# Sliding-window attention with sinks, then a mixture of four experts, on one core: the first q and k rows read in runs of four tokens, turned by transposes of 64x64, and the order of issue refitted

## The chip, the cores and the metric

The kernel runs on one core of a Trainium2 chip. The metric is the device time of one execution in microseconds; the kernel before takes 358.95 us (median of 3 runs, 358.85 to 359.42).

## What is computed

Four batches, eight heads, 768 tokens, head dimension 64. Each query sees the 128 latest keys and the first four tokens (the sinks). The attention output is laid out as 3072 tokens by 512 and goes through four experts, each a matrix of 512 by 1024, a ReLU and a matrix of 1024 by 512, mixed by normalized gates.

```python
scores = scale * np.matmul(q, k.transpose(0, 1, 3, 2))
keep = is_sink | ((rel >= 0) & (rel < window))      # rel = query position - key position
a = softmax(np.where(keep, scores, -1e9))
x = (a @ v).transpose(0, 2, 1, 3).reshape(B * S, H * D)
p = domain_probs / (domain_probs.sum(-1, keepdims=True) + 1e-09)
for e in range(E):
    out += p[:, e:e + 1] * (np.maximum(x @ w1[e], 0.0) @ w2[e])
```

## The kernel before

**Work.** A batch is cut into three groups of 256 tokens (g = 0, 1, 2) and a group's heads into four pairs (hp = 0 to 3). For each pair and group the attention of batch 0 runs through these steps: `transposes` (q and k turned so that the head dimension lies on the partitions, L594 to L600, and copied from PSUM to qkT, L613), `scores` (L706, in group 0 with a mask added by a matmul with the identity, L700), the exponential on ScalarE (L746), `values` (L786, sinks L779), reciprocal and scaling on VectorE (L813, L816), and `turn` (L847), which puts the tokens' features back on the partitions as xT. Later batches are turned by DMA transposes instead. The experts' first products take xT and w1 (L1106, for the first groups; L1189, in a form with seven products instead of eight, for the rest), their second products H and w2 (L1433, and L1358 in the seven-product form).

**First rows.** `load_first` (L287) reads group 0 of batch 0 as fp32: four DMAs of 256 KB, two for q on SP's queue and two for k on ACT's. Each takes four heads; partition p holds tokens 2p and 2p+1 of each head, so a packet is 512 bytes. `cast_first` (L308) casts each half to bf16 in the tiles `first`, q on VectorE and k on ScalarE (both recorded at L302). For hp 0 and 1 the first half is enough, hp 2 and 3 need the second. `transposes` turns, for each hp, 128 partitions by 128 columns (two heads of 64) for each of q and k and each of the two token parities: four transposes of 128x128, written to two PSUM banks (one for q, one for k), then one copy on VectorE (q) and one on ScalarE (k) that puts the tokens back in order.

**Other loads.** All other rows of batch 0, the values tiles vx and the weights are read by GpSimd's software DMA queue, in the order vx 0 and 1, q and k rows of group 1, vx 2, the first quarter of w1 of expert 0, vx 3, the other quarters, w2 of expert 0, and so on (L521 to L531). SP's queue also carries the gate probabilities (L457, L505) and the values of the sinks (vsf, L502, eight small DMAs).

**Start of the other engines.** VectorE and ScalarE first make the identity, and the masks (L535 to L565; ScalarE's two activations L544 and L545 make a term of the second mask, and a table load stands ahead of them). TensorE runs idle products (L574, into an accumulator that is not used yet) from its first instruction on: nine of 512 columns (L1464), and then one of 256 columns whenever the planner sees nothing ready within 220 ns (L1550).

**Order.** The order of all instructions is fixed when the program is built, by a planner that keeps an assumed clock for each engine (`t`, L108) and the assumed landing times of DMAs (`landed`). In each round (L1494) it picks the next TensorE work from options with priorities, and puts the other engines' work into a list with a ready time and an allowed delay (`later`, L163), from which `flush` (L167) emits it. The landing times of the first rows are numbers written out in `load_first` (L298), the times at which VectorE and ScalarE come free are set at L548. The block of constants from L60 to L113 holds the priorities, delays and shares: for example `GATE` and `GATE0` (allowed delay of the gated ReLU), `FORM` and `FORM2` (of the sums of weights for the seven-product form), `LOW_PRODUCT`, `HIGH_PRODUCT`, `LOW_SECOND`, `EARLY` and `OPEN` (priorities), `SHARE_OF` and `LEAD` (how far the attention of a batch runs ahead of the experts), `FLIP` (a delay put on transposes of groups 1 and 2).

Of the kernel before, what the change touches and what calls it, by code (L numbers as in the profile page):

```python
# [11 lines left out]
FP32 = mybir.dt.float32  # L12
BF16 = mybir.dt.bfloat16
# [3 lines left out]
def kernel(  # L17
# [12 lines left out]
    nc = tc.nc  # L30

    B, H, S, D = q.shape
# [5 lines left out]
    P = 128  # L38
# [6 lines left out]
    NQB = S // P  # L45
    NHP = H // 2
# [5 lines left out]
    G = 2 * P  # L52
# [5 lines left out]
    ]  # L58

    NGATE = 5  # L60
    START = {0: (1, 0), 1: (0, 1), 2: (0, 0), 3: (0, 0)}
    DENSE = 2
    NT3 = 3
    MIX = 4
    SHARE_OF = (0.634, 1.111, 1.102)
    LEAD = (1.272, 0.235)
    DUE = 0
    LOW_PRODUCT = 2.791
    LOW_SECOND = 4.402
    HIGH_PRODUCT = 0.207  # L70
    EARLY = 0.154
    GATE = 8921
    GATE0 = 5401
    FORM = 20576
    FORM2 = 37391
    TOKEN00 = 33179
    TOKEN0 = 1119
    WAIT2 = 16164
    WAIT1 = 5898
    LATE3 = 3  # L80
    TOKEN = 11155
    MARGIN = 494
    FULL = 7
    STEP0 = 0.141
    READY = 46
    WIDE = 2
    OPEN = 1.198
    ONACT = 1
    ONE = 2
    PAIR = 1  # L90
    SINK2 = 1
    PAD = 198
    MASKD = 99999999
    GROW = 24662
    ONLY2 = 1
    BEHIND = 7198
    CHORES = 2
    OWN = 2
    BIASED = 1
# [8 lines left out]
    t = {"pe": 1200.0, "act": 0.0, "dve": 0.0, "pool": 1280.0, "sp": 800.0, "sw": 6500.0, "hw": 0.0}  # L108
    ring, whole = [0.0] * 6, [False] * 6
    WARM = 6600.0  # L110
    FLIP = 421
    LATE = 259
    LATE1 = 12449  # L113

    def pe(cols, *deps, n=1, switch=0):
        t["pe"] = max([t["pe"], *deps])
        rate = 2.4 if t["pe"] > WARM else 1.2
        t["pe"] += cols / rate + 2.5 * n + 95 * switch
        return t["pe"] + 215
# [47 lines left out]
    def flush(until, once=False):  # L167

        ran = False
        while True:  # L170
            best = None
            for engine in ("act", "dve", "pool"):
                mine = [x for x in pend if x[2] == engine or x[2] == "any" and engine != "pool"]
                if not mine:
                    continue
                at = max(t[engine], min(x[0] for x in mine))
                if at <= until and (best is None or at < best[0]):
                    best = at, engine, min((x for x in mine if x[0] <= at), key=lambda x: x[1])
            if best is None:
                return ran  # L180
            pend.remove(best[2])
            t[best[1]] = best[0]
            best[2][3](best[1])
            ran = True
            if once:
                return True
# [14 lines left out]
    landed = {}  # L201
# [32 lines left out]
    sb = ctx.enter_context(tc.tile_pool(name="attn_sb", bufs=2))  # L234
    mo = ctx.enter_context(tc.tile_pool(name="moe_sb", bufs=2))
# [9 lines left out]
    nat = {}  # L245
# [40 lines left out]

    def load_first():  # L287

        raw = {name: mo.tile([P, 2, 4, 2 * D], FP32, name=f"{name}raw", tag=f"wide{i}", bufs=1) for i, name in enumerate("qk")}
        for half in range(2):  # L290
            hs = slice(4 * half, 4 * half + 4)
            for name, src in (("q", q), ("k", k)):
                x = raw[name][:, half]
                (nc.sync if name == "q" else nc.scalar).dma_start(
                    out=x, in_=src[0, hs, 0:G, :].rearrange("h (p t) d -> p h (t d)", t=2),
                )
                nat[0, half, name, "raw"] = x
            landed["first", half] = ((4870.0, 5180.0), (7550.0, 7350.0))[half]  # L298
            t["sp"] += 530

    def copy(engine, out, in_):
        (nc.scalar.copy if engine == "act" else nc.vector.tensor_copy)(out=out, in_=in_)  # L302

    first = {name: sb.tile([P, 2, H, D], BF16, name="qkn", tag="qkn", bufs=NQB) for name in "qk"}
    qkn_free[-2:] = [1e12] * 2
    cast_at = {}

    def cast_first(half):  # L308
        hs = slice(4 * half, 4 * half + 4)

        def cast(at):
            cast_at[half] = at

        part = join(2, cast)
        for i, name in enumerate("qk"):
            def run(engine, i=i, name=name):
                copy(
                    engine, first[name][:, :, hs, :],
                    nat[0, half, name, "raw"].rearrange("p h (t d) -> p t h d", t=2),
                )  # L320
                part(clock(engine, 512))
            later(("dve", "act")[i], landed["first", half][i], 0, run)
# [130 lines left out]
    pr = scratch[:, 4 * P:4 * P + E * NT].rearrange("p (j e) -> p j e", e=E)  # L453
# [46 lines left out]
    for h in range(H):  # L500
        r = 32 * (h // 2) + NSINK * (h % 2)
        nc.sync.dma_start(  # L502
            out=vsf[r:r + NSINK, :, 0:D], in_=v[:, h, 0:NSINK, :].rearrange("b j d -> j b d"),
        )
    nc.sync.dma_start(out=pr, in_=moe_domain_probs.rearrange("(p j) e -> p j e", p=P))  # L505
    ident = consts.tile([P, P], BF16, name="ident")
    for sgn in (1, -1):
        nc.gpsimd.affine_select(
            out=identf, in_=identf, compare_op=ALU.is_ge, fill=0.0,
# [5 lines left out]
    for base, sgn in ((0, 1), (NSINK - 1, -1)):  # L515
        nc.gpsimd.affine_select(
            out=sel2, in_=sel2, compare_op=ALU.is_ge, fill=0.0, base=base,
# [10 lines left out]
    for i in range(1, 4):  # L528
# [11 lines left out]
        out=low[0].rearrange("p (n q) -> p n q", n=3)[:, 0::2], in0=two, scalar1=LOW, scalar2=-LOW, op0=ALU.mult, op1=ALU.add,  # L540
# [4 lines left out]
    nc.scalar.activation(out=low[1][:, P:2 * P], in_=own, func=AF.Copy, scale=LOW, bias=-LOW)  # L545
    mask0 = consts.tile([P, 3 * P], BF16, name="mask0")
    mask1 = consts.tile([P, 2 * P], BF16, name="mask1")
    t["dve"] = t["act"] = 4600.0  # L548
    cast_first(0)
    flush(4700.0)  # L550
    for x in vx:
        nc.vector.memset(x[:, :, D:DX], 1.0)
    t["dve"] += 240.0

    vsd = {}
    half = consts.tile([P, 2], BF16, name="half")
# [6 lines left out]
        nc.vector.memset(x, 0.0)  # L563
    for x, y in zip((mask0, mask1), low):
        nc.vector.tensor_scalar(out=x, in0=y, scalar1=1 / LOW, scalar2=1.0, op0=ALU.mult, op1=ALU.add)  # L565
    t["dve"] += 400.0
    cast_first(1)

    acc = [psum.tile([P, 2 * G], FP32, name=f"acc{i}", tag=f"o{i}", bufs=1) for i in range(2)]

    def idle_products(x, n, cols=2 * G):

        for _ in range(n):
            nc.tensor.matmul(x[:, 0:cols], lhsT=zeros[:, 0:P], rhs=zeros[:, 0:cols], start=True, stop=True)  # L574
            pe(cols)
# [5 lines left out]
    def transposes(b, g, hp):  # L581

        if b not in qkT:
            qkT[b] = sb.tile([P, 2, NHP, S], BF16, name="qkT", tag="qkT", bufs=1)
        ready = max(cast_at[hp // 2] if (b, g) == (0, 0) else rows_at(b, g), free_at(2 if (b, g) == (0, 0) else 1))
        slots, trs = [], []
        for i in range(2 if (b, g) == (0, 0) else 1):
            slots.append(pick())
            trs.append(bank(slots[i], [P, 2, 2, P], BF16, "tr"))
            ring[slots[i]] = 1e12  # L590
        hs = slice(2 * hp, 2 * hp + 2)
        for i in range(2):
            for tt in range(2):
                if (b, g) == (0, 0):  # L594
                    nc.tensor.transpose(trs[i][:, i, tt], first["qk"[i]][:, tt, hs], ident)
                    continue
                for ph in range(2):
                    nc.tensor.transpose(
                        trs[0][64 * ph:64 * ph + 64, i, tt], nat[b, 2 * g + i][:, 2 * hp + ph, tt * D:(tt + 1) * D], ident,
                    )  # L600
        done = pe(4 * P, ready, n=4, switch=0 if (b, g) == (0, 0) else 2)
        dst = qkT[b][:, :, hp, g * G:(g + 1) * G]

        def copied(at):
            for slot in slots:
                take(slot, at)
            turned_at[b, g, hp] = at

        if (b, g) == (0, 0):
            part = join(2, copied)  # L610
            for i, engine in enumerate(("dve", "act")):
                def run(engine, i=i):
                    copy(engine, dst[:, i].rearrange("c (p t) -> c p t", t=2), trs[i][:, i].rearrange("c t p -> c p t"))  # L613
                    part(clock(engine, 2 * P))
                later(engine, done, 0, run)
        else:
            def run(engine):
                copy(engine, dst.rearrange("c i (p t) -> c i p t", t=2), trs[0].rearrange("c i t p -> c i p t"))
                copied(clock(engine, 4 * P))
            later("any", done, 300, run)  # L620
        if hp == NHP - 1:
            for _ in range(2):
                qkn_free.remove(1e12)
                qkn_free.append(done)
            qkn_free.sort()
# [835 lines left out]

    idle_products(acc[1], 9)  # L1464
    mix = Mixture()
    att = Attention(0)
    work = [
# [2 lines left out]
    ahead, upto, loaded, wide = 0, 0.0, 0, 0  # L1470
# [23 lines left out]
    while mix.more() or att.more():  # L1494
        now = t["pe"]

        if not att.more() and ahead == B - 1 and not wide:
            wide = 1
# [16 lines left out]
        x = next((x for x in loads if load_ready(x) < now + 1500), None)  # L1515
# [3 lines left out]
        if turns and (ahead < 2 or not mix.second) and landed.get(("qk", *turns[0]), 1e12) < now and (turns[0][0] <= ahead or turns[0][0] == ahead + 1 and not att.todo):  # L1519
            x = turns.pop(0)  # L1520
            turn_nat(*x)
            b = x[0]
# [18 lines left out]
        s2, p = mix.second_ready(), mix.product_ready()  # L1541
# [10 lines left out]
        if soonest > 1e11:  # L1552
            if loads:
                x = loads.pop(0)
# [50 lines left out]
```

## Time and profile before

| | us |
|---|---|
| median of 3 runs | 358.95 |
| the profiled execution's own time | 358.95 |
| its span, first to last instruction | 357.2 |
| TensorE busy | 348.8 (98%) |
| VectorE busy | 306.7 (86%) |
| ScalarE busy | 168.7 (47%) |
| GpSimd busy | 70.5 (20%) |
| first transposes of the first rows start (L595) | 5.83 |
| values tiles 0 and 1 landed | 8.28, 9.32 |
| last matmul starts | 353.18 |

The profile shows one execution. Its page gives each engine's busy time, the span in 40 slices, the DMA queues, the chain of work that ended last and the costliest groups of instructions; further views answer for a stretch of time, a line or a tile. The granted clock of TensorE is 1.00 throughout. PE is TensorE's matmuls, PEld its weight loads, DVE VectorE, ACT ScalarE, POOL GpSimd, SP the engine that only issues DMAs. Packet and completion times come from the same trace: q0 is GpSimd's software queue, q1 SP's and q10 ACT's hardware queue. The largest shares of the chain that ended last are the experts' products: 35% at L1189, 31% at L1358 and 7% at L1433.

### The profile page before, as it was taken

To read this page: it belongs to the slowest core of one execution; us is meant where nothing else is said; L and a number is where in the kernel's file an instruction comes from. 1 tells how busy PE (TensorE), PEld (TensorE's weight loads), DVE (VectorE), ACT (ScalarE), POOL (GpSimd) and SP (SyncE) were. 2 spreads that over 40 slices of the span, in tenths; PEclk is the share of its full clock that TensorE was granted. 3 is DMA by queue.
4 is the path that set the end of the run, shared out by engine and by line. 5 is a ranking of instruction groups with operands and counts; after the bars stand their busy time and mean duration, and the time that the engine had idled before them with its cause. 6 is when DMAs were issued, how large, how long until landed. Compare 5 with 4: busy or idle time off the path is not lost.

```text
span 357.2 us, 11108 instructions
## 1 busy us (share of the span) xinstructions
PE 348.8 (98%) x4673; PEld 302.6 (85%) x4673; DVE 306.7 (86%) x701; ACT 168.7 (47%) x432; POOL 70.5 (20%) x90
## 2 busy tenths in 40 slices
PE   8999999999999999999999999999999999999995
PEld 3675687777688998998998998899899999999884
DVE  6669999998799899899699799699799699999630
ACT  5866451437882922566444722926443632322110
POOL 8934114311260440420030620000000000000000
PEclk9999999999999999999999999999999999999999
DMA  9999999999993999691086999124112221100011
GB/s 175 185 195 203 230 210 174 137 135 139 227 148 42 138 168 157 75 119 46 32 68 111 148 156 139 50 54 55 44 32 63 59 52 51 37 31 31 1 61 60
DMA packets 115318, 37.86 MB, mean 106 GB/s; under 512 B 97196, under 2 KB 110764, under 8 KB 115268
## 3 DMA queue, kind: packets, MB, share of 16 engines
q0 software_dynamic: 74416, 17.31, 55.4%
q1 hardware_dynamic: 39796, 19.32, 29.3%
q8 instruction: 36, 0.59, 0.7%
q10 hardware_dynamic: 1056, 0.52, 0.6%
q14 instruction: 14, 0.11, 0.1%
HBM read 41.03 MB, written 6.34 MB: 133 GB/s over the span
## 4 chain that ended last, share of the span: by engine, by line
PE 83%; DVE 6%; ACT 5%; DMA 2%; issue 1%; POOL 1%; DVEq 0%
PE cps L1189 35%; PE acc L1358 31%; PE acc L1433 7%; PE hps L1106 3%; PE sps L706 3%; ACT onat L825 2%; PE od L786 2%; ACT aT L746 2%; DMA vx<-in_v_dram 2%; DVE H L1223 1%; DVE cps L1239 1%; DMA gates<-gate_rows 1%; PE od L779 1%; DVE onat L816 1%; DVE H L1254 1%
## 5 line engine op out<-in xcount | busy, mean ns | idle before, releaser
L1189 PEld LDWEIGHTS <-w 128*128 128x128 bf16 x1408 | 87.1, 98 | 3.5 <-issue 1.0
L1358 PEld LDWEIGHTS <-H 128*128 128x128 bf16 x720 | 66.6, 98 | 7.9 <-issue 1.2
L1223 DVE SCALAR_TENSOR_TENSOR H<-cps,gates 128x512 bf16<-128x512 f32 x105 | 69.8, 683 | 0.0
L1358 PE MATMUL acc<-w,H 128*128 128x256 bf16 x432 | 56.8, 273 | 0.1
L1189 PE MATMUL cps<-xT,w 128*128 128x128 bf16 x704 | 52.5, 219 | 0.5 <-ACT onat L825 0.5
L1189 PE MATMUL cps<-T,w 128*128 128x128 bf16 x704 | 52.5, 219 | 0.1
L746 ACT ACTIVATE aT<-sps 128x512 bf16<-128x512 f32 (+1 forms) x96 | 46.5, 571 | 9.7 <-PE sps L706 9.5
L1232 ACT COPY cps<-cps 128x512 f32<-128x512 f32 x44 | 25.7, 592 | 44.2 <-PE cps L1189 33.8
L1405 ACT COPY osb<-acc 128x256 f32<-128x256 f32 x40 | 15.4, 384 | 59.2 <-PE acc L1358 59.2
L825 ACT ACTIVATE onat<-od,R 128x64 bf16<-128x64 f32 x144 | 32.8, 349 | 21.7 <-DVE R L813 21.7
L1358 PE MATMUL acc<-wf,H 128*128 128x256 bf16 x288 | 39.3, 273 | 0.0
L1189 PEld LDWEIGHTS <-qkn 128*128 128x128 bf16 x576 | 34.8, 98 | 1.1 <-issue 0.2
L1239 DVE TENSOR_TENSOR cps<-H,cps 128x512 f32<-128x512 f32 x40 | 27.7, 691 | 9.0 <-PE cps L1189 6.2
L1358 PEld LDWEIGHTS <-S 128*128 128x128 bf16 x320 | 30.2, 98 | 4.2 <-issue 1.0
L1245 ACT COPY H<-cps 128x512 f32<-128x512 f32 x40 | 23.7, 600 | 18.1 <-PE cps L1189 18.1
L1433 PE MATMUL acc<-w,H 128*128 128x512 bf16 x128 | 30.1, 379 | 0.0
L1189 PEld LDWEIGHTS <-vf 128*128 128x128 bf16 x480 | 28.8, 98 | 0.1
L331 POOL DMA_DIRECT2D vx<-in_v_dram x24 | 21.4, 909 | 37.4 <-PE od L786 25.9
L1254 DVE TENSOR_TENSOR H<-H,cps 128x512 f32<-128x512 f32 x40 | 27.0, 680 | 1.7 <-PE cps L1189 1.6
L271 POOL DMA_DIRECT2D rows<-in_q_dram x18 | 16.0, 887 | 61.1 <-DMA qkT<-rows 51.0
L1189 PE MATMUL cps<-T,qkn 128*128 128x128 bf16 x384 | 27.3, 219 | 0.1
L727 DVE TENSOR_TENSOR aT<-aT,mask 128x1024 bf16<-128x1024 bf16 (+1 forms) x36 | 22.8, 641 | 1.9 <-ACT aT L746 1.6
(123 smaller groups left out, 524.2 us busy)
## 6 DMA issues: line engine op xcount, KB each, us to landing
w<-in_moe_w_dram POOLq DMA_DIRECT2D x7, 1024.0 KB, 23.1
out_dram<-osb SPq DMA_DIRECT2D x23, 256.0 KB
gates<-gate_rows SPq DMA_DIRECT2D x40, 128.0 KB
vx<-in_v_dram POOLq DMA_DIRECT2D x24, 128.0 KB, 10.0
rows<-in_q_dram POOLq DMA_DIRECT2D x18, 128.0 KB, 6.4
rows<-in_k_dram POOLq DMA_DIRECT2D x18, 128.0 KB, 6.7
w<-in_moe_w_dram POOLq DMA_DIRECT2D x4, 256.0 KB, 8.4
kraw<-in_k_dram ACTq DMA_DIRECT2D x2, 256.0 KB
```

The lines of the kernel that those rows point to most:

```text
L331: nc.gpsimd.dma_start(out=vx[tb][:, :, 0:D], in_=v[b, :, tb * P:(tb + 1) * P, :].rearrange("h p d -> p h d"),)
L727: nc.vector.tensor_mul(x, x, m[:, None, :].to_broadcast([P, n, 2 * w // n]))
L746: nc.scalar.activation(out=a[:, ph], in_=sps[ph][:, 0:w], func=AF.Exp, scale=scale)
L825: nc.scalar.mul(o[:, qi, hp, ph * D:(ph + 1) * D], od[:, qi, ph, 0:D], R[:, qi, ph])
L1189: nc.tensor.matmul(y[:, f], lhsT=A[:, d, f * P:(f + 1) * P], rhs=T[:, d], start=(m in ("P1", "P5") and f == 0 and d == 0), stop=(d == 1), ...
L1223: nc.vector.scalar_tensor_tensor(out=dst, in0=src, scalar=0.0, in1=gate, op0=ALU.max, op1=ALU.mult)
L1232: nc.scalar.copy(out=tiles["Y"], in_=y)
L1239: nc.vector.tensor_add(tiles["V"], c5, tiles["X"])
L1245: nc.scalar.copy(out=c5, in_=y)
L1254: nc.vector.tensor_add(c5, c5, y)
L1358: nc.tensor.matmul(x, lhsT=self.operand(b, g, e, m)[:, f], rhs=forms[e][m][:, f], start=(k == 0 and f == 0 and m in (("P1", "P5", "P2") if ...
L1433: nc.tensor.matmul(op, lhsT=H[:, fb // QF, fb % QF, s], rhs=w2_sb[e][:, fb, :], start=(fb == 0), stop=(fb == NFB - 1),)
```

## The change

The first rows are read in runs of four tokens: partitions 0 to 63 take the even heads of the half and partitions 64 to 127 the odd ones, partition p of a half holding tokens 4p to 4p+3. Each DMA therefore covers 64 partitions and two heads, with packets of 1024 bytes, and there are eight instead of four. The casts copy without a change of order. For each hp, each of q and k is turned by eight transposes of 64x64, two (one on each half of the partitions) for each of the four tokens of a run, in the same two PSUM banks; the copies after them put four tokens in order instead of two. The casts of the first half are entered in the planner's list after the masks, its assumed landing times and engine times are new constants (`FIRST`, `BEGIN`), the idle products at the start become six (`NIDLE`), and some 25 of the planner's other constants get new values.

```diff
+    RUN = 4
+    FIRST = ((3980.0, 3950.0), (5500.0, 5450.0))
+    BEGIN = (4400.0, 4000.0)
+    NIDLE = 6
...
-    SHARE_OF = (0.634, 1.111, 1.102)
-    LEAD = (1.272, 0.235)
+    SHARE_OF = (0.61, 1.111, 1.102)
+    LEAD = (1.272, 0.328)
...
-    LOW_PRODUCT = 2.791
-    LOW_SECOND = 4.402
-    HIGH_PRODUCT = 0.207
-    EARLY = 0.154
-    GATE = 8921
-    GATE0 = 5401
+    LOW_PRODUCT = 2.872
+    LOW_SECOND = 4.475
+    HIGH_PRODUCT = 0
+    EARLY = 0.207
+    GATE = 9087
+    GATE0 = 5108
...
-    FORM2 = 37391
+    FORM2 = 43794
...
-    FLIP = 421
+    FLIP = 34
...
-        raw = {name: mo.tile([P, 2, 4, 2 * D], FP32, ...) ...}
+        raw = {name: mo.tile([P, NHP, RUN * D], FP32, ...) ...}
         for half in range(2):
             hs = slice(4 * half, 4 * half + 4)
             for name, src in (("q", q), ("k", k)):
-                x = raw[name][:, half]
-                (nc.sync if name == "q" else nc.scalar).dma_start(
-                    out=x, in_=src[0, hs, 0:G, :].rearrange("h (p t) d -> p h (t d)", t=2),
-                )
+                x = raw[name][:, 2 * half:2 * half + 2]
+                rows = src[0, hs, 0:G, :].rearrange("(n h) (p t) d -> h p n (t d)", h=2, t=RUN)
+                for ph in range(2):
+                    (nc.sync if name == "q" else nc.scalar).dma_start(out=x[64 * ph:64 * ph + 64], in_=rows[ph])
...
-            landed["first", half] = ((4870.0, 5180.0), (7550.0, 7350.0))[half]
+            landed["first", half] = FIRST[half]
+            t["sp"] += 530
             t["sp"] += 530
...
-    t["dve"] = t["act"] = 4600.0
-    cast_first(0)
-    flush(4700.0)
     for x in vx:
         nc.vector.memset(x[:, :, D:DX], 1.0)
-    t["dve"] += 240.0
...
-    t["dve"] += 400.0
+    t["dve"], t["act"] = BEGIN
+    cast_first(0)
     cast_first(1)
...
+            if (b, g) == (0, 0):
+                x = trs[i][:, i].rearrange("c t p -> c (t p)").rearrange("c (t p) -> c t p", t=RUN)
+                for tt in range(RUN):
+                    for ph in range(2):
+                        pr = slice(64 * ph, 64 * ph + 64)
+                        nc.tensor.transpose(x[pr, tt], first["qk"[i]][pr, hp, tt], ident[pr, pr])
+                continue
             for tt in range(2):
-                if (b, g) == (0, 0):
-                    nc.tensor.transpose(trs[i][:, i, tt], first["qk"[i]][:, tt, hs], ident)
-                    continue
...
-                    copy(engine, dst[:, i].rearrange("c (p t) -> c p t", t=2), trs[i][:, i].rearrange("c t p -> c p t"))
+                    x = trs[i][:, i].rearrange("c t p -> c (t p)")
+                    copy(engine, dst[:, i].rearrange("c (p t) -> c p t", t=RUN), x.rearrange("c (t p) -> c p t", t=RUN))
...
-    idle_products(acc[1], 9)
+    idle_products(acc[1], NIDLE)
```

The other constants that move, old value first: TOKEN0 1119, 1517; WAIT2 16164, 15046; WAIT1 5898, 5930; TOKEN 11155, 12447; MARGIN 494, 154; FULL 7, 8; STEP0 0.141, 0.15; READY 46, 17; OPEN 1.198, 0.991; GROW 24662, 24255; BEHIND 7198, 7891. The planner also counts two changes of TensorE's tile shape for the first transposes, which it counted as none.

More of the change, by code (lines that the diff above doesn't have):

```diff
@@ L64 @@
     MIX = 4
-    SHARE_OF = (0.634, 1.111, 1.102)
-    LEAD = (1.272, 0.235)
+    SHARE_OF = (0.61, 1.111, 1.102)
+    LEAD = (1.272, 0.328)
     DUE = 0
-    LOW_PRODUCT = 2.791
-    LOW_SECOND = 4.402
-    HIGH_PRODUCT = 0.207
-    EARLY = 0.154
-    GATE = 8921
-    GATE0 = 5401
+    LOW_PRODUCT = 2.872
[4 more added lines that the diff above has]
+    GATE0 = 5108
     FORM = 20576
-    FORM2 = 37391
+    FORM2 = 43794
     TOKEN00 = 33179
-    TOKEN0 = 1119
-    WAIT2 = 16164
-    WAIT1 = 5898
+    TOKEN0 = 1517
+    WAIT2 = 15046
+    WAIT1 = 5930
     LATE3 = 3
[L81 to L85, printed above, removed]
+    TOKEN = 12447
+    MARGIN = 154
+    FULL = 8
+    STEP0 = 0.15
+    READY = 17
     WIDE = 2
-    OPEN = 1.198
+    OPEN = 0.991
     ONACT = 1
@@ L93 @@
     MASKD = 99999999
-    GROW = 24662
+    GROW = 24255
     ONLY2 = 1
-    BEHIND = 7198
+    BEHIND = 7891
     CHORES = 2
@@ L287, in load_first @@
     def load_first():
-        raw = {name: mo.tile([P, 2, 4, 2 * D], FP32, name=f"{name}raw", tag=f"wide{i}", bufs=1) for i, name in enumerate("qk")}
+        raw = {name: mo.tile([P, NHP, RUN * D], FP32, name=f"{name}raw", tag=f"wide{i}", bufs=1) for i, name in enumerate("qk")}
         for half in range(2):
@@ L302, in copy @@
         (nc.scalar.copy if engine == "act" else nc.vector.tensor_copy)(out=out, in_=in_)
-    first = {name: sb.tile([P, 2, H, D], BF16, name="qkn", tag="qkn", bufs=NQB) for name in "qk"}
+    first = {name: sb.tile([P, NHP, RUN, D], BF16, name="qkn", tag="qkn", bufs=NQB) for name in "qk"}
     qkn_free[-2:] = [1e12] * 2
@@ L308, in cast_first @@
     def cast_first(half):
-        hs = slice(4 * half, 4 * half + 4)
         def cast(at):
@@ L317, in run @@
                 copy(
-                    engine, first[name][:, :, hs, :],
-                    nat[0, half, name, "raw"].rearrange("p h (t d) -> p t h d", t=2),
+                    engine, first[name][:, 2 * half:2 * half + 2],
+                    nat[0, half, name, "raw"].rearrange("p h (t d) -> p h t d", t=RUN),
                 )
@@ L600, in transposes @@
                     )
-        done = pe(4 * P, ready, n=4, switch=0 if (b, g) == (0, 0) else 2)
+        done = pe(4 * P, ready, n=4, switch=2)
         dst = qkT[b][:, :, hp, g * G:(g + 1) * G]
```

## Prediction

> **What bounds the kernel now.** I read the page first, its busy times and its slices:
>
> ```profile
> PE 348.8 (98%) x4673; PEld 302.6 (85%) x4673; DVE 306.7 (86%) x701; ACT 168.7 (47%) x432; POOL 70.5 (20%) x90
> ...
> PE   8999999999999999999999999999999999999995
> ```
>
> TensorE is filled from the first slice to the last; the reader is to see that a change can win only where PE is idle, late to start, or fed with fillers. PE is idle for 357.2 - 348.8 = 8.4 us. The table of windows puts 1.85 of it in 0 to 10 us, 0.40 in 10 to 20, 0.85 in 20 to 30, 0.27 in 30 to 40, 3.55 after 300 (nearly all of it the last store, behind the last matmul) and about 1.5 over the 260 us between. To this come the fillers of L574: 21 matmuls, 1.92 us before 5 us and 1.28 between 5 and 16, if counted at the later rate (L1433: 512 columns in 216 ns). So the head is where the change can act, and I asked for the chain of waits of the first 30 us alone:
>
> ```profile
> 2.53 0.99 POOL vx L331
> 3.52 5.80 DMA vx<-in_v_dram
> 9.36 0.26 PE od L786 x3
> ...
> 22.29 0.44 DVE onat L816
> 22.77 0.30 PE tx L847 x2
> 23.09 0.38 ACT xT L302
> 23.52 2.45 PE hps L1106 x21
> ```
>
> Columns: start, length, what. The head is a chain that starts with a software DMA (the first two values tiles, landing at 9.32), runs over VectorE and ScalarE, and gives the bound to PE only at 23.5. The timeline shows the other input, the first q and k rows:
>
> ```profile
> 1.94 1.28 ACT L544 ACT_TABLE_LOAD   x1 [1.94 <-issue]
> ...
> 4.48 0.43 DVE L302 CAST qkn<-qraw 128x512 bf16<-128x512 f32 x1
> ...
> 4.93 0.62 ACT L302 CAST qkn<-kraw 128x512 bf16<-128x512 f32 x1 [1.19 <-DMA kraw<-in_k_dram]
> ...
> 5.83 0.61 PE L595 MATMUL tr<-ident,qkn 128*128 128x128 bf16 x8
> ...
> 6.81 0.57 DVE L302 CAST qkn<-qraw 128x512 bf16<-128x512 f32 x1
> 7.03 0.62 ACT L302 CAST qkn<-kraw 128x512 bf16<-128x512 f32 x1
> ```
>
> The k casts start as their rows land (4.91 and 7.00, from the completions in the trace). The first q cast starts as VectorE comes free (masks until 4.46; q landed at 4.46). The second q rows landed at 6.11, and their cast stood behind two copies. Last, the windows of half a microsecond (columns: length, busy time of each engine, clock, DMA share, GB/s):
>
> ```profile
> 2.00:2.50 0.50, 0.50 (x3) 0.15 (x1) 0.47 (x2) 0.50 (x1) 0.43 (x3) 1.00 0.51 116
> 2.50:3.00 0.50, 0.50 (x2) 0.15 (x1) 0.39 (x4) 0.50 (x1) 0.50 (x2) 1.00 0.59 154
> ...
> 3.50:4.00 0.50, 0.50 (x3) 0.21 (x2) 0.42 (x5) 0.25 (x2) 0.50 (x2) 1.00 1.15 344
> ...
> 5.50:6.00 0.50, 0.50 (x8) 0.45 (x7) 0.00 (x0) 0.05 (x1) 0.50 (x1) 1.00 1.30 298
> ```
>
> The rows come slowly for the first microsecond, then at 344 GB/s; the last packet starts at 6.08. The first software packet starts at 5.78, though GpSimd issued it at 2.49. Later in the trace, where that queue had been empty, the first packet came 1.6 to 2.2 us after the issue. So the values wait for the first rows to get off the 16 DMA engines, and from then on the software stream has no gap until 89 us.
>
> **The change, part by part.**
>
> *Rows in runs of four tokens.* 2048 packets of 512 B become 1024 of 1024 B. In this trace hardware packets of 512 B take 27 ns at best, other ones of 1024 B (stores, gates) 44 at the lower quarter and 49 at the median. At best: 2048 x 27 / 16 = 3.46 us against 1024 x 44 / 16 = 2.82, 0.64 saved. In the slow first microsecond the packets come at 226 to 268 per us, and only the SP queue's until 2.86; if packets and not bytes are what is limited there, doubling their size moves those 135 KB in half the time, 0.4 saved. Bounds: 0 (344 GB/s is a limit of bytes, and the ramp is time) to 1.2. I take 0.9, near the sum, since the ramp's rows are so far under the later ones: last packet at about 5.2.
>
> *Eight issues instead of four.* SP and ACT each issue two more. An issue of 512 packets took 0.45 to 0.58, one of 16 packets (vsf) 0.25 to 0.30, a store of 128 packets 0.34; the new ones carry 128, so I take 0.36. ACT: 4 x 0.36 = 1.44 for 1.10, so the table load and the two activations behind it come 0.35 later and end at 4.1. Behind them VectorE's last mask waits: it began at 3.86 and took 0.60, to 4.46, and GpSimd's issue ended at 4.43, so it may well have waited for that. Up to 0.4 on ACT is then free. At 0.55 an issue, ACT ends at 4.85 and mask and q cast slip by 0.7 or more: that end is kept for the range. On SP the two issues stand ahead of the probabilities and vsf, and these will wait for semaphores of the first rows as the vsf issues already do (3.0 us for kraw). Their readers come at 13.9 (vsd) and 25.9 (gates), issues end at 8.4 now: nothing, with 5 us of cover.
>
> *First half.* The q cast cannot start before 4.46, as now; the k cast starts at 4.1 instead of 4.93. Both are over by 4.9 instead of 5.55. The idle products must not stand in the way: nine of 512 columns at 0.43 us end near 5.3, six end at 4.0, and the planner adds short ones up to the rows. First transposes 5.83 to about 5.05: 0.8 earlier.
>
> *Transposes of 64x64.* 64 instead of 16. The 16 start 56 ns apart. The nearest row for small ones is L598 (64 columns loaded, 128 moved): 0.64 us for 16, the last 0.22 being latency, 28 ns apart. 64 x 28 = 1.8 us for 0.9; between 25 and 56 ns apart it is +0.7 to +2.7 us of PE, partly in idle time. A change of shape ahead of L706 costs about 0.25 of weight-load idle (4.5 us in 18); I allow two or three more. On the chain that is 0.2 to 0.3 for each half.
>
> [...]
>
> *Second half and copies.* Rows land near 5.9 instead of 7.0. The casts then stand behind the first copies, not behind the DMA, and end about 6.5 instead of 7.65. hp 2 and 3 are scored a microsecond earlier, so the first values wait for vx alone. The copies keep their size (0.37 to 0.43).
>
> *Software stream.* It starts as the rows leave the engines: 5.78 less 0.9, no earlier than 2.49 + 2.2 = 4.7. GpSimd issues far ahead (5.8 us from issue to landing at first, 9.2 at the last w1 piece), so vx (9.32), w1 (14.61 to 19.36) and w2 (24.47) all come 0.9 earlier, and the pieces under PE's later work move with it.
>
> *Order.* Some 25 numbers of the planner move a little. Between 40 and 350 us PE is idle for only 1.5 us, so a new order can win at most about that; it can lose as much in stalls at the handovers between batches (near 98, 121 and 221 us the chain already leaves PE). I take 0, bounds -0.7 to +1.2.
>
> *Sum.* -0.9 (stream and rows) -0.5 (hp 2 and 3 no longer late) +0.3 (transposes on the chain) + 0 = -1.1 us of the profiled execution's 358.95 (span 357.2 and 1.75 around it), which is also the median of the runs shown: 357.85.
>
> **Rivals.**
>
> *A. The stream does not move, or the head's gain is given back.* If the first software packet at 5.78 is the queue's own start-up, vx stays at 9.32 and w1 where it is; only hp 2 and 3 gain, 0.2 to 0.4: 358.6. For it: the first k packet too came late, at 2.86. Against it: the 1.6 to 2.2 us of later issues. The same time results if VectorE (95% busy from 30 to 60 us) cannot follow.
>
> *B. Slower: pieces of 64 partitions at half rate.* If writes to one half of the partitions get half the engines' rate (344 / 2 = 172 GB/s), and q and k ask for the same half at once, 1.05 MB take 6.1 us, the last packet starts near 8 instead of 6.08, and the second rows land near 8.9. hp 2 and 3 slip by 1.9, the stream by 1 to 2. With 0.5 of the slip taken up by work at hand: about +1.2, 360.1. It decides as soon as the eight pieces average under 250 GB/s. Against it: k starts later than q, so the two may write different halves.
>
> [...] No row of this trace has such a piece, so it stays open here.
>
> *C. Slower: the new order stalls at a handover.* One more stall like those near 98 or 121 us (aT and onat on ACT, 1.6 and 2.5 long) with the head's 1.1 gained: +0.8 net, 359.8. Decides once PE idle between 40 and 350 us exceeds 1.5 by more than the head's gain.
>
> **How the numbers follow.** Forecast (-0.6 to -2.0): 0.58. A: 0.20. B: 0.08. C: 0.14. A time within 0.2% (0.72 us) is about what a measurement of this kernel cannot tell from no change; the edges are 358.23 and 359.67. Nearly all of the forecast lies below, A between, B and C above mostly: 0.58 faster, 0.22 same, 0.20 slower. The forecast's own range is 356.9 to 358.3; with A and part of C, 356.7 to 359.8 leaves out less than 2 in 10.
>
> **What would show it.** Right: kraw completions near 4.0 and 5.9, first software packet near 4.9, first 64x64 transposes near 5.05, vx at 8.4, first hps products of the second group (22.89 now) before 22. Wrong: a first packet still at 5.8 (A), second rows after 7 (B), the q cast after 5 (the issues), PE idle over 2.5 us between 40 and 350 (C).

## The result, and the profile after

The kernel after takes 363.59 us (median of 5 runs, 362.81 to 363.88) against 358.95 for the kernel before (5 runs, 358.55 to 359.42): a ratio of 1.012, 95% interval 1.0106 to 1.0134. That is 4.6 us slower, where 1.1 us faster was forecast and 356.7 to 359.8 was the range. The profiled execution has a span of 362.2 us for 357.2. The page of the kernel after:

```profile
PE 349.3 (96%) x4710; PEld 302.7 (84%) x4719; DVE 306.2 (85%) x701; ACT 169.1 (47%) x432; POOL 68.5 (19%) x90
...
PE   4898999999989999999999999999999999999996
...
PEclk9699999999999999999999999999999999999999
```

TensorE is busy for nearly as long as before (349.3 for 348.8), so 4.5 of the 5.0 us are idle time. The reader is to see the first slice at 4 (it was 8) and, what the page before did not have, a granted clock of 6 tenths in the second slice. Line numbers have moved: from the masked scores on they are higher by five (L711 is L706 of before), the helper of casts and copies is L307 (L302), the first transposes are L598 (L595). The chain of waits of the first 32 us (start, length, what):

```profile
3.15 6.51 DMA qraw<-in_q_dram
9.76 0.44 DVE qkn L307
10.24 0.64 PE tr L598 x16
10.88 0.75 PE sps L705 x2
...
14.44 0.45 PE od L791 x6
...
28.83 2.45 PE hps L1111 x21
```

The head no longer hangs on the values tiles but on the last piece of the first q rows. The first values products come at 14.37 in the timeline (8.85 before), and the products that end the head at 28.83 instead of 23.52: 5.3 us late. The last matmul starts at 358.78 instead of 353.18, so the loss is made in the head, and the rest adds 0.3. The timeline of the head:

```profile
3.52 1.28 ACT L547 ACT_TABLE_LOAD   x1 [3.52 <-issue]
...
6.42 0.87 DVE L307 CAST qkn<-qraw 128x512 bf16<-128x512 f32 x1 [0.84 <-DMA qraw<-in_q_dram]
...
7.34 0.69 PE L598 MATMUL tr<-ident,qkn 64*64 64x64 bf16 x32 [2.31 <-DVE qkn L307]
...
9.76 0.43 DVE L307 CAST qkn<-qraw 128x512 bf16<-128x512 f32 x1 [2.47 <-DMA qraw<-in_q_dram]
...
10.10 1.08 DVE L307 COPY qkT<-tr 128x256 bf16<-128x256 bf16 x3
...
10.81 0.82 PE L705 MATMUL sps<-lent,ident 128*128 128x384 bf16 x2
...
14.37 0.51 PE L791 MATMUL od<-vx,aT 128*128 128x65 bf16 x6
```

A mask product pair and the first values products of the kernel before, for comparison:

```profile
6.38 0.49 PE L700 MATMUL sps<-lent,ident 128*128 128x384 bf16 x2
...
8.85 0.25 PE L786 MATMUL od<-vx,aT 128*128 128x65 bf16 x3
```

Three things are to be seen. ScalarE's table load starts at 3.52 instead of 1.94. The rows come late: q casts at 6.42 and 9.76 instead of 4.48 and 6.81. And VectorE's copies of the first two pairs, turned by 8.0, start at 10.10: on VectorE they stand behind the second half's cast. Windows (length, busy times of PE, PEld, DVE, ACT and POOL, clock, DMA share, GB/s), first of the kernel before, then two of the kernel after:

```profile
5.00:10.00 5.00, 4.56 (x47) 2.57 (x45) 2.32 (x7) 3.88 (x10) 5.00 (x7) 1.00 1.97 193
```

```profile
5.00:10.00 5.00, 0.72 (x33) 0.58 (x32) 1.33 (x3) 1.56 (x5) 4.42 (x6) 0.79 1.85 183
10.00:15.00 5.00, 4.76 (x52) 1.84 (x54) 1.26 (x5) 3.19 (x9) 3.31 (x5) 0.53 1.85 177
```

From 5 to 10 us TensorE has 0.72 us of work (4.56 before). From 10 to 15 it looks busy, at half its clock: two mask products take 0.82 us (L705) where they took 0.49 (L700).

The clock column needs a warning. The trace's clock entries are 1.00 from 4.50 us, 0.50 from 7.91 and 1.00 again from 14.73. They begin with the first change, and for the time before it the views count 1.00, which the matmuls contradict: idle products of 512 columns start 0.43 us apart there, and such products 0.22 apart later (L1433 of before). So TensorE started at half rate in both kernels, and the 1.00 throughout of the kernel before holds from 5.56 us on, where its entries begin.

The DMAs of the first rows, from the completions and packets in the traces (KB of 1024 bytes, by the packets begun):

| kernel | DMAs x partitions, packet | one issue, us | KB moved by 5.0 us | last half q, k landed |
|---|---|---|---|---|
| before | 4 x 128, 512 B | 0.45 to 0.58 | 772 | 6.11, 7.00 |
| after | 8 x 64, 1024 B | 0.62 to 0.83 | 563 | 9.67, 9.31 |
| e1 (k's halves swapped) | 8 x 64, 1024 B | 0.62 to 0.83 | 605 | 9.11, 8.84 |
| e2 (other tokens) | 8 x 128, 1024 B | 0.40 to 0.46 | 908 | 7.34, 7.57 |
| e3 (before, halves) | 8 x 64, 512 B | 0.63 to 0.84 | 537 | 10.19, 9.62 |
| e4 (before, eight) | 8 x 128, 512 B | 0.45 to 0.53 | 706 | 7.36, 7.67 |
| e7 (before, even and odd) | 8 x 64 in steps of two, 512 B | 0.62 to 0.84 | 490 | 8.46, 8.03 |

Each row is one execution. How far such figures scatter is shown by runs that share their loads: with those of the kernel after, e6, e8, e10 and e11 moved 610, 599, 578 and 556 KB by 5.0 us, and their last rows landed at 9.47, 9.20, 9.38 and 9.83. With those of e2, e12 and e13 moved 734 and 825 KB and ended at 8.03 and 7.81.

### The profile page after: what moved, and what is told of

It reads as the page before. It is cut to its first block, busy times and chain, and to the rows that moved or that the text cites. A ratio compares the mean times of both kernels' runs of the same rounds, so it can differ in the third digit from the quotient of the medians.

```text
span 362.2 us, 11203 instructions
## 1 busy us (share of the span) xinstructions
PE 349.3 (96%) x4710; PEld 302.7 (84%) x4719; DVE 306.2 (85%) x701; ACT 169.1 (47%) x432; POOL 68.5 (19%) x90
## 4 chain that ended last, share of the span: by engine, by line
PE 87%; ACT 4%; DVE 4%; DMA 3%; issue 1%; SPq 1%; DVEq 0%
PE cps L1194 37%; PE acc L1363 32%; PE acc L1438 7%; PE sps L711 3%; PE hps L1111 3%; PE od L791 2%; ACT onat L830 2%; DMA qraw<-in_q_dram 2%; DMA xT<-onat 1%; ACT aT L751 1%; PE od L784 1%; PE sps L705 1%; DVE onat L821 1%; SPq L300 1%; PE tx L852 1%
## 5 line engine op out<-in xcount | busy, mean ns | idle before, releaser
L1438 PE MATMUL acc<-w,H 128*128 128x512 bf16 x119 | 29.0, 379 | 0.6 <-issue 0.2
L1228 DVE SCALAR_TENSOR_TENSOR H<-H,gates 128x512 bf16<-128x512 f32 x35 | 23.7, 680 | 0.0
```

The costliest lines, as they stand in the source:

```text
L1228: nc.vector.scalar_tensor_tensor(out=dst, in0=src, scalar=0.0, in1=gate, op0=ALU.max, op1=ALU.mult)
L1438: nc.tensor.matmul(op, lhsT=H[:, fb // QF, fb % QF, s], rhs=w2_sb[e][:, fb, :], start=(fb == 0), stop=(fb == NFB - 1),)
```

## The experiments

All ratios are against the kernel before, run on the same chip beside them (358.86 to 359.04 us). The first five ask why the rows are late.

**e1_swap.** In the kernel after, k's pieces are issued in the other order, so that q and k aim at opposite halves of the partitions.

```diff
-                for ph in range(2):
+                for ph in range(2) if name == "q" else (1, 0):
```

> The kernel after, with k's two pieces of each half issued in the other order (odd heads, partitions 64 to 127, first), so that SP's and ACT's pieces aim at opposite halves of the partitions. Theory H (pieces of 64 partitions that aim at the same half share half the rate; after: 1.05 MB from 2.3 to 8.5 us): rows move at 250 to 340 GB/s, the last piece lands at 6.3 to 7.0 instead of 9.67, and the time falls to 359.5 to 361. Theory N (the eight issues of 0.62 to 0.83 us and small DMAs are what is slow): last landing within 0.4 us of 9.67, time 363 to 364. Theory K (packets of 1024 bytes are slow): as N.

Measured: 363.60 us, 1.0131 (1.011 to 1.0153). Packets took 63 ns in the mean between 3 and 5 us instead of 77 (68 to 74 in the other runs with the loads of the kernel after), but only 605 KB had come by 5.0, inside the 556 to 610 of those loads, and the last rows landed at 9.11, just ahead of their 9.20 to 9.83. So my form of H, two queues that share one half, falls: relieving the half gains nothing clear of the scatter.

**e2_full128.** Each of the eight DMAs reaches all partitions; it reads one head's first 512 tokens, so the first rows hold other tokens.

```diff
-                    (...).dma_start(out=x[64 * ph:64 * ph + 64], in_=rows[ph])
+                    (...).dma_start(
+                        out=x[:, ph], in_=src[0, 4 * half + ph, 0:2 * G, :].rearrange("(p t) d -> p (t d)", t=RUN),
+                    )
```

> The kernel after, but each of the eight DMAs reads one head's first 512 tokens over all 128 partitions (128 packets of 1024 bytes, as many bytes and issues as before it); so the first rows hold other tokens and the output isn't the reference's. H: each piece reaches all partitions, the last lands at 5.8 to 6.6, time 358.5 to 360.5. N: landing near 9.7 and 363 to 364, since number and size of the DMAs stay. K: the same as N, since the packets stay.

Measured: 360.99 us, 1.007 (1.0042 to 1.0098), single executions from 360.1 to 363.4 with mean clocks from 1.000 to 0.991. The bytes by 5.0 us rise to 908 KB and the issues are short: N and K fall, and 64 partitions are what is slow. But H's own figures are missed too: the rows land at 7.57, half a microsecond behind the kernel before, and 2.0 us remain (1.2 in the profiled execution, 360.25 us, whose clock does not fall again once it is full). The timeline of TensorE says where:

```profile
5.59 1.06 PE L600 MATMUL tr<-ident,qkn 64*64 64x64 bf16 x32 [0.17 <-DVE qkn L309]
8.10 0.53 PE L600 MATMUL tr<-ident,qkn 64*64 64x64 bf16 x16 [1.44 <-DVE qkn L309]
8.56 0.50 PE L707 MATMUL sps<-lent,ident 128*128 128x384 bf16 x2
```

The first two pairs are turned by 6.7 (at half rate still: the 32 took 1.06 us, those of e12 0.69, and the clock entries begin at 6.84), and nothing of them is scored until the third pair's rows have come.

**e3_before_halves.** The kernel before with its own order, each first load cut into partitions 0 to 63 and 64 to 127.

```diff
+                for ph in range(2):
+                    (...).dma_start(
+                        out=x[64 * ph:64 * ph + 64],
+                        in_=src[0, hs, P * ph:P * ph + P, :].rearrange("h (p t) d -> p h (t d)", t=2),
+                    )
```

> The kernel before, with each of its four first loads cut into two of 64 partitions (packets of 512 bytes, the same rows, order of issue and constants of before). H: the same half rate, last landing at 8.5 to 10 instead of 7.0; the order of before lets the first half's copies and scores go ahead of the second casts, so the time rises by 1.5 to 3.5 to 360.5 to 362.5. N: the same landing. K: landing near 7.0 and 359, since packets are as before.

Measured: 360.60 us, 1.0042 (1.0027 to 1.0057). The rows land at 10.19, later than in the kernel after, and yet only 1.6 us are lost. Its clock stayed full from 4.74 us on, through idle stretches of TensorE of 1.8 and 1.3 us. Its timeline shows the order of before at work, scores of the first pairs ahead of the late cast:

```profile
7.97 0.49 PE L702 MATMUL sps<-lent,ident 128*128 128x384 bf16 x2
...
10.28 0.43 DVE L304 CAST qkn<-qraw 128x512 bf16<-128x512 f32 x1 [1.80 <-DMA qraw<-in_q_dram]
```

**e4_before_eight.** The kernel before with eight first loads of two heads each, all over 128 partitions.

```diff
+                for i in range(2):
+                    (...).dma_start(
+                        out=x[:, 2 * i:2 * i + 2],
+                        in_=src[0, 4 * half + 2 * i:4 * half + 2 * i + 2, 0:G, :].rearrange("h (p t) d -> p h (t d)", t=2),
+                    )
```

> The kernel before, with each of its four first loads cut into two of two heads over all 128 partitions (512 bytes a packet, 256 packets a DMA): eight issues without the halves. H: last landing within 0.7 of 7.0, and the time moves only by what two more issues ahead of ACT's table load cost, 0 to 1.0: 359 to 360. N: landing at 8.5 to 10 and 360.5 to 362.5, as the run with halves. K: 359.

Measured: 358.64 us, 0.9986 (0.9977 to 0.9996), rows at 7.67. Eight issues cost nothing here; it is the fastest version that computes the reference's rows, if by less than 0.2%.

**e7_before_interleave.** The kernel before with pieces of 64 partitions that take every second one.

```diff
+                rows = src[0, hs, 0:G, :].rearrange("h (p e t) d -> e p h (t d)", e=2, t=2)
+                for e in range(2):
+                    (...).dma_start(out=x[e::2], in_=rows[e])
```

> The kernel before with each first load cut into two of 64 partitions, the even and the odd ones (so each piece reaches over the whole range of partitions), the same rows and packets. H (pieces confined to one half of the partitions are slow): last landing at 7.2 to 8.2 as with eight pieces over 128, 358.4 to 359.3. Theory I (any piece of 64 partitions is slow to generate, 0.62 to 0.83 us an issue): issues of that length, landing at 9 to 10 and 360.2 to 360.9, as with the halves.

Measured: 359.49 us, 1.002 (1.0009 to 1.0031), issues of 0.62 to 0.84 us, rows at 8.46. Between the two forecasts: against e4 the 64 partitions cost about 1 us wherever they lie (0.85 by the medians, 1.2 by the ratios; long issues, 490 KB by 5.0 us), and e3's half in one block costs about another (1.1 by the medians, 0.8 by the ratios; rows at 10.19, packets of 36 ns in the mean between 3 and 5 us instead of 32).

The other runs ask where the rest of the 4.6 us is.

**e5_before_neworder.** The kernel before with the 21 refitted constants alone (LEAD, SHARE_OF, LOW_PRODUCT and the others listed above).

> The kernel before with the 21 refitted constants of the planner and nothing else (its own loads, transposes, landing times and nine idle products). Theory P (what is lost beside the slow pieces is lost by the order of the head, planned for rows that land at 5.5): the refit alone is worth 0.5 at most, 358.5 to 359.5. Theory O (the refitted order stalls later on): 360.5 or more.

Measured: 358.78 us, 0.9991 (0.9982 to 1.0000). The refit by itself does no harm in the kernel before; there O falls.

**e6_replan.** The kernel after with landing and engine times as measured.

```diff
-    FIRST = ((3980.0, 3950.0), (5500.0, 5450.0))
-    BEGIN = (4400.0, 4000.0)
+    FIRST = ((6700.0, 6450.0), (10000.0, 9700.0))
+    BEGIN = (5900.0, 5600.0)
```

> The kernel after with the planner's assumed landing and engine times set to those measured in it (casts at 6.7, 6.45, 10.0 and 9.7, engines free at 5.9 and 5.6). The planner then puts the first half's copies and scores ahead of the second casts and more idle products ahead of the transposes. P: 360.3 to 361.5, about what the halves cost in the kernel before (360.6). O, or a theory that the 64x64 transposes cost the time: above 362.5.

Measured: 368.91 us, 1.028 (1.0253 to 1.0308): 5.3 us slower still, where P forecast a gain; the time falls on the side of O. In the head it did what P says, the first values products came at 10.61 instead of 14.37. But the assumed times enter every later choice. From 15 to 20 us TensorE has 3.49 us of work (4.71 in the kernel after), and from 100 to 120 it has 15.77 (18.78); at 19.8 and at 108.6 its clock fell to 0.50 for 3.4 us. Its waits (who, for whom: us in all, times, longest):

```profile
PE acc L1363 <- DVE S L1309: 4.1, 3, 2.9
PE sinks L672 <- POOL ksd L635: 1.4, 1, 1.4
```

So this run doesn't test P: it changed the whole order. The test has to move the head's instructions and leave the planner alone, as the next ones do.

**e8_warm.** The kernel after with 18 idle products of 256 columns ahead of the transposes of the first and of the third pair, outside the planner's account.

```diff
+        if (b, g) == (0, 0) and hp % 2 == 0:
+            for _ in range(18):
+                nc.tensor.matmul(acc[1][:, 0:G], lhsT=zeros[:, 0:P], rhs=zeros[:, 0:G], start=True, stop=True)
```

> The kernel after with 18 more idle products of 256 columns ahead of the first and ahead of the third pair's transposes, where TensorE stood idle for 2.3 and 2.2 us. Theory W (the granted clock falls to 0.50 from 8 to 14.5 us since TensorE idles, and the work in that stretch takes twice as long): clock 1.00 throughout and 360.8 to 362.3. If the clock is of no account there, since VectorE and ScalarE set the pace: 363 to 364.

Measured: 361.76 us, 1.0072 (1.0056 to 1.0089), mean clock 1.00 in each run; in the profiled one the clock entries begin, with 1.00, at 7.25 us. Work that does nothing makes the kernel 1.8 us faster: W holds. The third pair was turned at 10.96, later than in the kernel after, and the first values products came at 13.44 instead of 14.37.

**e10_held.** The kernel after; the second half's casts, the third pair's transposes and their copies are kept back until the third pair's scores, with the planner's account unchanged.

```diff
-                copy(engine, first[name][...], nat[...])
+                held_back.append(cast_now) if half else cast_now()
...
+                held_back.append(turn_now) if hp == 2 else turn_now()
...
+                    held_back.append(copy_now) if hp == 2 and held_back else copy_now()
...
     def scores(b, hp, g, more=False):
+        if hp >= 2:
+            release()
```

> The kernel after with its planner and loads untouched, but the second half's casts, the third pair's transposes and their copies are put out only ahead of the third pair's scores, so that the first two pairs' copies and scores no longer stand behind rows that land at 9.7. Theory P (the order of the head turns the late rows into a stall of everything): scores of pairs 0 and 1 near 8.5 instead of 11.6, TensorE warm again by the third pair, time 360.8 to 362.0. If the rows alone set the end: 363 or more.

Measured: 363.09 us, 1.0113 (1.0095 to 1.0131): a miss, only 0.4 of the 1.6 to 2.8 expected; the time falls on the side of the rows alone. The order did change; TensorE's timeline:

```profile
8.33 0.82 PE L720 MATMUL sps<-lent,ident 128*128 128x384 bf16 x2
...
10.71 0.77 PE L606 MATMUL tr<-ident,qkn 64*64 64x64 bf16 x16
```

The scores begin at 8.33 instead of 10.81. But TensorE had idled from 5.4 to 7.34, and everything up to 17 us runs at half rate (0.82 for two mask products). The view of the granted clock says 1.00 for this execution, since its clock entries begin only at 16.98: TensorE never reached the full clock before. The other three executions have a mean clock of 0.989 to 0.991, so they lost it too. That the half rate ate the gain is what the next run tests.

**e11_held_warm.** The same with 18 more idle products ahead of the first transposes.

> The run before with 18 more idle products of 256 columns ahead of the first transposes (none later). P and W together (order and clock): 360.2 to 361.2, near the 360.6 that the halves cost in the kernel before; what is left over 359 is then the slow pieces. Without W: as the run before.

Measured: 361.00 us, 1.0055 (1.0040 to 1.0070). The same lines of its timeline:

```profile
8.27 0.48 PE L723 MATMUL sps<-lent,ident 128*128 128x384 bf16 x2
...
10.41 0.44 PE L609 MATMUL tr<-ident,qkn 64*64 64x64 bf16 x16 [0.68 <-DVE qkn L307]
```

Order and clock together are worth 2.5 us (4.6 less 2.1 left); alone they gave 0.4 and 1.9, and the difference is within the noise. Most of it is the clock: 1.9 alone and 2.1 with the order mended, both clear of the noise, against 0.4 and 0.6 for the order, which are not.

**e12_full128_held and e13_full128_held_warm.** The kernel of e2 (other tokens) with the second half kept back as in e10; e13 has six more idle products ahead of the first transposes.

> The kernel after with both mended: each first load over 128 partitions (one head's first 512 tokens, other tokens than the reference's, as many bytes and issues), and the second half's work put out behind the first two pairs' scores. P: the 2.0 us that were left with full pieces go for the most part, 358.6 to 359.8. If the 64x64 transposes or the refit cost what is left: 360.5 or more.

> The run before with six more idle products of 256 columns ahead of the first transposes; it reads the same other tokens. P and W: 358.2 to 359.2 and clock 1.00 in every run, at or a little under the kernel before; the part of the change that remains then (packets of 1024 bytes, 64x64 transposes, refit) is worth about -0.5 to +0.2.

Measured: 359.33 us, 1.0010 (0.9999 to 1.0022), and 359.23 us, 1.0011 (0.9999 to 1.0023). The timeline of e12:

```profile
6.43 0.48 PE L722 MATMUL sps<-lent,ident 128*128 128x384 bf16 x2
...
10.09 0.36 PE L808 MATMUL od<-vx,aT 128*128 128x65 bf16 x6
```

With pieces over all partitions the rows come soon enough that TensorE hardly idles (0.35 us at most in e12), and the extra idle products change nothing. Against e2 the order is worth 1.5 us here, in part perhaps through the clock, of which a fall is on record in five of e2's seven executions and in none of these. The 358.2 to 359.2 expected of e13 is just missed: even with pieces, order and clock mended, the change gains nothing.

The parts, from e11 and e13 (one chip, 358.86 before): the pieces 361.00 - 359.23 = 1.8 us, order and clock 2.5, and 0.4 that is left (interval -0.04 to 0.8). They add up to the 4.6 because each is a difference of the same runs. The same pieces cost 1.6 in the kernel before (e3), which is a second measurement of that part.

## Why the prediction was wrong

- **Rows in runs of four tokens** is the step that failed first: -0.9 was forecast, the last rows came 2.7 us later. It took the piece's 64 partitions as free. They are what costs, about 1 us by their number and about 1 more by lying in one half (e4, e7, e3). The price of a packet was about right over 128 partitions (median 46 ns for 1024 bytes in e2, 44 taken), but the gain worked out from it did not come even there: the last rows of e2, e12 and e13 landed at 7.57, 8.03 and 7.81, those of e4, with 512 bytes and as many DMAs, at 7.67.
- **Rival B** had this with a chance of 0.08 and put the rows at 8.9 (9.67 measured) and the loss at 1.2 (1.6 and 1.8 measured). Its reason was not quite the measured one. That writes to one half of the partitions get half the rate was assumed, and no run shows it; and q and k asking for opposite halves changed little: e1 moved 605 KB by 5.0 us, inside the 556 to 610 of the loads of the kernel after, and its last rows landed at 9.11, just ahead of their 9.20 to 9.83. With no row of a piece of 64 partitions in the trace of before and only a guess against B, that the two may write different halves, 0.08 was far too little.
- **Eight issues**: 0.36 us each was taken, between rows of 16 and of 512 packets; 0.62 to 0.83 were measured. The number of packets does not explain it (e3's 256 packets and the 128 of the kernel after take the same); pieces of 64 partitions took longer than pieces of 128, the very first too (SP's 0.74 us, 0.40 in e2). It is not only a DMA's own shape: the first one of the gate probabilities, the same in all kernels, took 0.62 behind the pieces of 64 and 0.37 in e2. The bound of 0.55 was no bound. The table load slipped by 1.6 us and the second mask to 5.36. The q cast, foreseen at 4.5 and after 5 at worst, waited longer for its rows (6.42), and the first transposes came at 7.34 instead of 5.05.
- **Second half and copies** is the second failed step. It said that the casts would stand behind the first copies. The planner had put the casts first, since it assumed the rows at 5.5 and 5.45 (`FIRST`), before the first copies could be ready. The numbers were in the diff, and with rows at 9.7 this holds up the scores of all pairs, from 8.3 to 10.8 (e10). In the kernel after that alone is worth 0.4 to 0.6 us, not clear of the noise; it also makes the second of TensorE's two idle stretches. The prediction asked only what was late, not what was queued behind it.
- **The clock** was no term of the sum and no rival, and it is as large a part of the loss as the pieces. The idle products ended at 5.03, planned for rows at 3.98 (`FIRST`; with later times e6 filled the stretch); TensorE idled to 7.34 and again from 8.03 to 10.24, and its clock was at 0.50 from 7.91 to 14.73. That is worth 1.8 us alone (e8). The prediction had both rates in hand, idle products at 0.43 us at the start and the same length at 0.216 later, and did not ask what keeps the faster one.
- **Transposes of 64x64**: +0.3 was taken, at 28 ns each. At full clock 16 take 0.44 us with 0.22 of latency, 15 ns apart in the mean, so 64 cost 0.9 us as the 16 large ones did. The estimate took the transposes one by one. In the trace the two of a pair, one on each half of the partitions, write one bank and start 3 to 4 ns apart, the next pair 28 to 29 ns later.
- **Software stream**: the first packet came at 5.33 (4.9 forecast), but vx landed at 9.83 and 11.11, as the stream now shares the engines with rows whose last packet starts at 8.53. Where the rows were quick (e2), it started at 4.99 and vx 1 landed at 9.23.
- **Order**: 0 was taken with -0.7 to +1.2; e5 gives -0.25 us (interval -0.65 to 0) in the kernel before. Right, and C's sign, more than 2.5 us of idle PE between 40 and 350 us, did not show. That idle time is 2.0 us in the kernel after and 1.3 before (the prediction read 1.5); with the head mended it is 1.1 (e11), and with the old order and late rows 1.9 (e3), so it goes with the head and not with the refit.

## What to carry to other kernels

Look at the partitions that each piece of a DMA reaches before counting its packets: here pieces of 64 cost 1.8 us (e11 less e13), and longer packets were to save 0.9. Where the order is fixed in advance, read the times that it assumes and ask of every late input which instructions of its engine stand behind it. And where idle work holds up TensorE's clock, as here (1.00 in each run of e8, 0.991 in four of five of the kernel after), the price of a late input can be its wait and a half-rate stretch behind it: two idle stretches of 2.3 and 2.2 us came with one of 6.8. A granted clock of 1.00 in a view should be set against the lengths of the matmuls.

## What was not expected of the hardware

- An issue on SP's or ACT's queue took 0.40 to 0.46 us for 128 packets over 128 partitions (e2) and 0.62 to 0.83 for 128 packets over 64 (the kernel after).
- Two 64x64 transposes, one on each half of the partitions and both into one PSUM bank, started 3 to 4 ns apart, and the next two 28 to 29 ns later (kernel after, 7.42 to 7.84 us, granted clock 1.00).
- TensorE started at half rate: idle products of 512 columns start 0.43 us apart at first (before and after) and such products 0.22 apart later. In thirteen of these fourteen traces the full clock came at 4.1 to 7.3 us; in e10's, where TensorE had idled from 5.4 to 7.34, it came at 16.98. The views count 1.00 up to there, while two mask products took 0.82 us for 0.48.
- Apart from the last one of each trace, the clock entries last 3.41 us or whole multiples of it: 351.57 in the kernel before, 3.41, 6.83 and 348.16 in the kernel after.
- Why a piece of 64 partitions took longer to issue (0.62 us and more in the kernel after, 0.40 to 0.46 in e2), and why q's and k's pieces on opposite halves (e1) gained nothing clear, the runs do not show.
